# Linear attention and an FFT mixing block on one core: batch 0's DFT without folding, q maxima split in PSUM, V scaled in one tile, key-value copies per pair

## The chip, the cores and the metric

The kernel runs on one core of a Trainium2 chip. A core has five engines that run side by side, each through a queue of its own: TensorE (matmuls; PE in the profile, its weight loads PEld), VectorE (DVE), ScalarE (ACT), GpSimd (POOL) and SyncE (SP, used here to issue DMAs). The metric is the device time of one execution in microseconds (us), the median over runs; less is better.

## The reference

For 8 batches of 8 heads, 576 rows and 64 features per head, the reference computes a linear attention with learned features, then a Fourier mixing and a feed-forward block over the 512 channels that the heads form:

```python
def phi(x):
    proj = np.einsum('bhsd,df->bhsf', x, w_phi)
    proj = proj - np.max(np.abs(proj), axis=-1, keepdims=True)
    return np.concatenate([np.exp(proj), np.exp(-proj)], axis=-1)
q_p, k_p = (phi(q), phi(k))
kv = np.einsum('bhsf,bhsd->bhfd', k_p, v)
z = np.sum(k_p, axis=2)
num = np.einsum('bhsf,bhfd->bhsd', q_p, kv)
den = np.einsum('bhsf,bhf->bhs', q_p, z)[..., None] + 1e-06
...
X = np.fft.fft(x, axis=1)
X = np.fft.fft(X, axis=2)
u = x + np.real(X).astype(np.float32)
mu = np.mean(u, axis=-1, keepdims=True)
var = np.mean((u - mu) ** 2, axis=-1, keepdims=True)
un = (u - mu) / np.sqrt(var + 1e-06)
ch = np.maximum(un @ w_ch1, 0.0) @ w_ch2
return (u + ch).astype(np.float32)
```

The real part of the two transforms is a product with a cosine table on both axes less a product with a sine table on both axes.

## The kernel before

A batch passes through these stages. The names are those of the profile.

- Loads (`KS`, `QS`, `VS`) are issued on POOL's queue, and transposing DMAs on SP's queue make `KT` and `QT` from them. Batch 0 is loaded by SP as float32 into rooms that W2b and HT use later, and TensorE transposes it (`pst`).
- Keys: `psk` is the projection of a pair of heads; ACT takes both exponentials (`KPp`, `KPn`) and DVE the largest magnitude of each row (`MK`). The shift by the maximum is not put into the exponentials of k but into V: POOL multiplies V by exp(MK) and by exp(-MK), into the tiles VCn and VCp (and V4N, V4P for the last 64 rows), whose 65th column holds the scale itself and so yields the denominator.
- Queries: `psh`, `ph` and `psn` are projections, `QPHP` and `QPHN` their exponentials. The maxima of q (`MQ`, from `psq`) enter by a factor on the result (`E2`) in batches 1 to 7. In batch 0 they are turned into rows by `turn_m` (split into three bfloat16 parts on DVE, one matmul `pt` against an identity) and added to the projection on TensorE before the exponential (`negative`).
- `kv` is the key-value product of one head, in PSUM; ACT copies it to `kvh`. `pn` is the product with the query features; the division puts the result into `X`, 128 rows by five groups by 512 channels.
- Folding (`folded`): sums and differences of rows and of channels, on DVE, into `R` and then `CEO`. They use the symmetry of cosine and sine, so that the DFT along rows (`psD`, 12 matmuls, and 3 of `px`) and along channels (`pu`, 12 matmuls) is a quarter of the full one. The sum with `X` stays in `X`.
- Normalising: `UN` is the centred row, `UT` its transpose (`put` on TensorE in batch 0, a DMA in the others). The feed-forward block follows: `psf` with ACT's `HT`, then `pso`, then the store.

The tables of sine and cosine (`SS`, `CS`, `SD`, `CD`) are made on the chip at the start: POOL and DVE reduce the angles, ACT takes the sine. ACT loads a table of functions whenever it changes between sine and exponential.

The order of all this is written out by hand. Each stage is a generator that yields after a step, and the string `PLAN` names with one letter after another whose next step is issued: F the feed-forward, M the mixing with its heads, D the folding, T the exponentials, P the maxima of q, R those of k, S the scaling of V, N and U the normalising, K, V and Q the loads, W the weights' loads, C and H the tables, Z the memsets, G and J the transposes of batch 0's k and q, Y the `stir` steps: four matmuls of ones into a tile that nobody reads (`idle`), fifteen such steps. Every engine runs its part in that order, so an instruction that waits holds all behind it on its engine. `PAIRS` is the order of head pairs in batch 0: outer (0 and 3) first, then inner.

PSUM is cut into three pools: `pj` with 2 tiles of two banks, `pk` with 1, `pb` with 3 of one bank.

## Time and profile before

| what | value |
|---|---|
| median of 3 runs | 417.63 us |
| lowest and highest run | 414.85 and 420.42 us |
| the profiled execution | 415.15 us |
| its span, first to last instruction | 413.4 us |
| mean granted TensorE clock in it | 0.995 |
| HBM read and written | 36.77 and 9.44 MB |

The span is what the trace covers, and all lines of the profile are of that one execution. Its page names the busy time of each engine, but a busy share says little when stages have different limits: the windows of 8 to 32, 32 to 51 and 51 to 403 us have to be read apart. In a row of a timeline stand the start, the duration, the engine, the line, the operation, the tile it writes and those it reads, and in brackets the idle time ahead with what ended it.

### The profile page before, as it was taken

To read this page: it belongs to the slowest core of one execution; us is meant where nothing else is said; L and a number is where in the kernel's file an instruction comes from. 1 tells how busy PE (TensorE), PEld (TensorE's weight loads), DVE (VectorE), ACT (ScalarE), POOL (GpSimd) and SP (SyncE) were. 2 spreads that over 40 slices of the span, in tenths; PEclk is the share of its full clock that TensorE was granted. 3 is DMA by queue.
4 is the path that set the end of the run, shared out by engine and by line. 5 is a ranking of instruction groups with operands and counts; after the bars stand their busy time and mean duration, and the time that the engine had idled before them with its cause. 6 is when DMAs were issued, how large, how long until landed. Compare 5 with 4: busy or idle time off the path is not lost.

```text
span 413.4 us, 10526 instructions
## 1 busy us (share of the span) xinstructions
PE 394.6 (95%) x4194; PEld 259.5 (63%) x4194; DVE 319.4 (77%) x662; ACT 303.8 (73%) x617; POOL 215.1 (52%) x279
## 2 busy tenths in 40 slices
PE   7898999989999989999899999999999999999994
PEld 3574577535856568566756577566856586658563
DVE  5979887999699867797689878888799768875101
ACT  6988999658958886688868886789758885544350
POOL 8997695774466753707658373649271343201000
PEclk9999899999999999999999999999999999999999
DMA  7999979898674899654965979757952141106103
GB/s 210 221 170 158 181 100 185 87 118 128 102 118 58 67 179 141 63 92 83 129 97 65 156 104 142 80 72 116 117 97 52 46 83 21 27 14 114 24 23 90
DMA packets 108520, 42.71 MB, mean 103 GB/s; under 512 B 82615, under 2 KB 103479, under 8 KB 108471
## 3 DMA queue, kind: packets, MB, share of 16 engines
q0 software_dynamic: 46272, 16.60, 37.1%
q1 hardware_dynamic: 61703, 24.85, 32.9%
q10 hardware_dynamic: 496, 0.59, 0.6%
q8 instruction: 33, 0.54, 0.5%
q14 instruction: 16, 0.13, 0.1%
HBM read 36.77 MB, written 9.44 MB: 112 GB/s over the span
## 4 chain that ended last, share of the span: by engine, by line
PE 69%; DVE 13%; DMA 8%; ACT 4%; POOL 3%; issue 2%; DVEq 0%; POOLq 0%; SPq 0%; ACTq 0%
PE psf L1207 29%; PE pso L1224 19%; DMA UT<-UN 4%; PE kv L853 3%; PE psD L1035 2%; PE psk L468 2%; DMA KT<-KS 2%; PE pu L1087 2%; DMA KS<-in_k_dram 2%; PE psq L522 2%; PE psh L563 1%; DVE MK L488 1%; PE pso L1250 1%; DVE cb L969 1%; DVE X L1077 1%
## 5 line engine op out<-in xcount | busy, mean ns | idle before, releaser
L1207 PE MATMUL psf<-UT,W1b 128*128 128x320 bf16 (+1 forms) x1024 | 141.1, 286 | 2.9 <-DMA UT<-UN 2.8
L1224 PE MATMUL pso<-W2b,HT 128*128 128x512 bf16 x496 | 120.5, 379 | 0.0
L1207 PEld LDWEIGHTS <-W1b 128*128 128x128 bf16 x1024 | 94.6, 98 | 30.9 <-issue 3.8
L1212 ACT ACTIVATE HT<-psf 128x320 bf16<-128x320 f32 x128 | 53.9, 444 | 25.7 <-PE psf L1207 19.5
L1224 PEld LDWEIGHTS <-HT 128*128 128x128 bf16 x496 | 45.2, 98 | 43.2 <-issue 0.4
L975 POOL TENSOR_TENSOR X<-cb,rd 128x640 f32<-128x640 f32 x28 | 35.1, 1254 | 52.9 <-DVE rd L973 29.6
L443 POOL TENSOR_TENSOR VCn<-VS,VCn 128x512 bf16<-128x512 bf16 x28 | 29.9, 1067 | 43.4 <-ACT VCn L438 36.6
L530 DVE TENSOR_REDUCE MQ<-psq 128x8 f32<-128x1024 f32 (+1 forms) x32 | 34.3, 1088 | 17.8 <-PE psq L522 17.4
L1230 DVE SCALAR_TENSOR_TENSOR X<-pso,rs,X 128x512 f32<-128x512 f32 x31 | 23.0, 743 | 28.2 <-PE pso L1224 28.0
L1214 ACT ACTIVATE HT<-psf 128x512 bf16<-128x512 f32 x64 | 37.3, 602 | 6.8 <-PE psf L1207 6.6
L488 DVE TENSOR_REDUCE MK<-psk 128x8 f32<-128x1024 f32 x28 | 33.8, 1210 | 1.4 <-ACT KPn L474 1.4
L474 ACT ACTIVATE KPp<-psk 128x1024 bf16<-128x1024 f32 x28 | 28.8, 1027 | 7.8 <-PE psk L468 7.5
L258 POOL DMA_DIRECT2D QS<-in_q_dram x49 | 33.4, 688 | 1.1 <-issue 1.1
L1133 ACT ACTIVATE UN<-X,MV 128x512 bf16<-128x512 f32 (+1 forms) x35 | 25.2, 726 | 11.5 <-DVE MV L1158 8.0
L572 ACT ACTIVATE QPHP<-psh 128x1024 bf16<-128x1024 f32 x28 | 28.9, 1031 | 4.8 <-PE psh L563 4.5
L474 ACT ACTIVATE KPn<-psk 128x1024 bf16<-128x1024 f32 x28 | 28.7, 1025 | 1.7 <-DVE MK L488 1.6
L443 POOL TENSOR_TENSOR VCp<-VS,VCp 128x512 bf16<-128x512 bf16 x28 | 29.9, 1067 | 0.0
L572 ACT ACTIVATE QPHN<-psh 128x1024 bf16<-128x1024 f32 x28 | 29.0, 1036 | 0.0
L1157 DVE BATCH_NORM_STATS2 st<-X 128x6 f32<-128x512 f32 (+1 forms) x40 | 27.1, 678 | 0.2
L1077 DVE TENSOR_TENSOR X<-pu,X 128x512 f32<-128x512 f32 (+3 forms) x49 | 23.5, 526 | 4.6 <-PE pu L1087 4.5
L955 PEld LDWEIGHTS <-QPHP 128*128 128x128 bf16 x280 | 20.5, 99 | 7.8 <-DVE cb L969 3.8
L1173 POOL TENSOR_TENSOR rs<-VE,mhalf 128x5 f32<-128x5 f32 (+1 forms) x9 | 10.3, 1148 | 24.8 <-DVE VE L1172 24.7
(462 smaller groups left out, 797.2 us busy)
## 6 DMA issues: line engine op xcount, KB each, us to landing
out_dram<-X SPq DMA_DIRECT2D x31, 128.0 KB
out_dram<-X SPq DMA_DIRECT2D x15, 256.0 KB
KS<-in_k_dram POOLq DMA_DIRECT2D x7, 512.0 KB, 8.2
VS<-in_v_dram POOLq DMA_DIRECT2D x14, 256.0 KB, 4.8
W1b<-in_moe_w_ch_dram POOLq DMA_DIRECT2D x1, 2048.0 KB, 15.3
W2b<-in_moe_w_ch_dram POOLq DMA_DIRECT2D x1, 2048.0 KB, 16.1
QS<-in_q_dram POOLq DMA_DIRECT2D x28, 64.0 KB, 3.6
QS<-in_q_dram POOLq DMA_DIRECT2D x7, 256.0 KB, 5.6
```

The source lines that it names most:

```text
L258: nc.gpsimd.dma_start(out=pieces[i][0], in_=pieces[i][1])
L443: nc.gpsimd.tensor_tensor(out=VC[:, hs, :, 0:D], in0=values[b][0][:, hs, :].rearrange("p h (j d) -> p h j d", d=D), in1=VC[:, hs, :, D:D + ...
L474: nc.scalar.activation(out=KP[:, hs, :, :].rearrange("p e (jp jj) f -> p jj (e jp) f", jj=2), in_=psk[:], func=AT.Exp, scale=sgn,)
L488: nc.vector.tensor_reduce(out=MK[:, 2 * pr:2 * pr + 2, :].rearrange("p e (jp jj) -> p jj (e jp)", jj=2), in_=tiles[pr][:], axis=AX.X, op=A ...
L530: nc.vector.tensor_reduce(out=o, in_=i[:], axis=AX.X, op=ALU.max, apply_absolute_value=True)
L572: nc.scalar.activation(out=o, in_=psh[:], func=AT.Exp, scale=sgn)
L975: nc.gpsimd.tensor_tensor(out=X[:, :, at:at + 2 * D].rearrange("p c (e d) -> p e c d", e=2), in0=cb[:, :, :, 0:D], in1=rd[:].to_broadcast( ...
L1077: nc.vector.tensor_tensor(out=to, in0=more, in1=to, op=ALU.add)
L1207: nc.tensor.matmul(ps, lhsT=W1b[:, cc, 128 * hh:128 * hh + 128], rhs=UT[:, cc, lo:hi], start=(cc == 0), stop=(cc == NCC - 1),)
L1212: nc.scalar.activation(out=HT[:, hh, lo:hi], in_=ps, func=AT.Relu, scale=-1.0)
L1214: nc.scalar.activation(out=HT[:, hh - 1:hh + 1, lo:hi], in_=psw[:].rearrange("p (a n) -> p a n", a=2), func=AT.Relu, scale=-1.0,)
L1224: nc.tensor.matmul(po[:], lhsT=HT[:, hh, at:at + 128], rhs=W2b[:, hh, :], start=(hh == 0), stop=(hh == NHH - 1),)
```

## The change

It has four parts, and the first half of `PLAN` is written anew for them; behind batch 2 the string is the same letter for letter.

- Batch 0's DFT is done without folding. `less_first` subtracts row 0 from `X` (a matmul `pm` of ones with that row, a subtraction on DVE), in two halves of the channels, into `XB` (bfloat16, in R's room). `first_rows` runs 40 matmuls of 320 columns (for each quarter of the channels, cosine and sine, five groups of rows), and `first_channels` 48 of 256 columns in place of 12. They need a few more tables, products of CD and SD with alternating signs (`full`, `SN`), made on DVE.
- The sines are taken at the start, ahead of the first exponential; the warm-up call of ACT loads the sine table. The angles are reduced on DVE, where POOL did a part. `PAIRS` is now 0, 1, 2, 3, and outer means heads 0 to 3; `stir` has seven steps.
- `turn_m` transposes the float32 maxima three times over in one go and takes the three bfloat16 parts out of PSUM.
- V, in all batches, is scaled into one tile for both signs (VC, V4S): POOL writes the negative of MK beside it, ACT takes one exponential over both, and POOL one product over both. `keyvalue` puts two heads into one PSUM tile, and ACT copies both at once.

On ACT, at the start of the program, the rows ahead of the first exponential of the keys (`KT` is the transposed k of batch 0, `K4p` and `K4n` the features of its last rows, `KPp` those of a pair) were:

```order
L357 CAST wphi_95<-wphi_f 128x128
L350 CAST KT_169<-pst 128x256
L350 CAST KT<-pst 128x512
L761 ACTIVATE K4p<-ps_229 128x512
L762 ACTIVATE K4n<-ps_229 128x512
L776 ACTIVATE KPp<-psk 128x2x4x128
```

and are:

```order
L383 CAST wphi_95<-wphi_f 128x128
L376 CAST KT_168<-pst 128x256
L376 CAST KT<-pst 128x512
L217 ACTIVATE SS<-gs 128x960
L221 ACTIVATE CS<-ga,halfpi 128x960
L226 ACTIVATE SD<-ga 128x512
L228 ACTIVATE CD<-ga,halfpi 128x512
L779 ACT_TABLE_LOAD
L779 ACTIVATE K4p<-ps_224 128x512
```

The four sines and the load of the exponential table moved ahead of batch 0's features; before they stood behind batch 0's last exponential, with a table load on either side:

```order
L690 ACTIVATE QPHN<-ph_739 128x2x2x64
L212 ACT_TABLE_LOAD
L212 ACTIVATE SS<-gs 128x960
L216 ACTIVATE CS<-ga,halfpi 128x960
L221 ACTIVATE SD<-ga 128x512
L223 ACTIVATE CD<-ga,halfpi 128x512
L882 CAST HI_103<-R 1x257
L883 CAST HI_103<-R 1x255
L459 ACT_TABLE_LOAD
```

At that place the last exponential is now followed by the copies of row 0 alone, and batch 1's keys come next.

On DVE, from the last division of batch 0's heads on (`X` is the attention's result), the rows were:

```order
L919 TENSOR_TENSOR X<-pn__794,rd_815 128x2x5x64
L869 TENSOR_TENSOR R<-X 128x2x256 x2
L875 TENSOR_TENSOR R<-X 128x255
L878 TENSOR_TENSOR R<-X 128x1
L875 TENSOR_TENSOR R<-X 128x255
L878 TENSOR_TENSOR R<-X 128x1
L886 TENSOR_TENSOR R<-R 128x2x255 x2
L890 TENSOR_TENSOR R<-R 128x2
L893 SCALAR_TENSOR_TENSOR R<-R 128x2
L998 SCALAR_TENSOR_TENSOR R<-R,keep,pm 65x257
```

and are:

```order
L934 TENSOR_TENSOR X<-pn__768,rd_789 128x2x5x64
L903 TENSOR_TENSOR R<-X,pm 128x2x256 x2
L907 SCALAR_TENSOR_TENSOR R<-X,keep,pm 65x256
L903 TENSOR_TENSOR R<-X,pm 128x2x256 x2
L907 SCALAR_TENSOR_TENSOR R<-X,keep,pm 65x256
L1077 CAST R<-psD 128x320
L520 TENSOR_REDUCE MK_727<-ps_811 128x4
```

The foldings are gone, six subtractions stand in their place, and the results of the row DFT (`psD`) are read out right behind them.

The core of the diff:

```diff
-PAIRS = (0, 3, 2, 1)
+PAIRS = (0, 1, 2, 3)
...
-    "CYCCZYCYGGTRTTGZZGTYZWRTJTSRJGRJYSTPTSPKTTPJMJRTSSKMYMBMPTQPTPQVTMZTMQTMMTPCMMMTTMTHDYAMMYHHDHHKYYVD"
+    "CCYCCGCGZHZHCHHTZGGTHJTKHPQTTJZKRWSRJYTTRGJSSPRTYPTRJTMMYPTSTMMPSTTZPTMPTBKZTMQMMQMHTTHMMVTAMMMDYDYD"
...
+    V4S = const.tile([128, 2, 4, 2, D + 1], BF16, name="V4S")
...
-        nc.scalar.activation(out=warm[:], in_=halfpi[:], func=AT.Exp)
+        nc.scalar.activation(out=warm[:], in_=halfpi[:], func=AT.Sin)
...
+    def scaling(b, MK, MK4, VC):
...
+        def scale_v(pr):
+            if pr % 2 == 0:
+                h4 = slice(2 * pr, 2 * pr + 4)
+                nc.gpsimd.tensor_single_scalar(
+                    out=MK[:, 0, h4], in_=MK[:, 1, h4], scalar=-1.0, op=ALU.mult
+                )
+                nc.scalar.activation(
+                    out=VC[:, :, h4, :, D].rearrange("p s h j -> p s (h j)"),
+                    in_=MK[:, :, h4].rearrange("p s h j -> p s (h j)"), func=AT.Exp, scale=1.0,
+                )
+            hs = slice(2 * pr, 2 * pr + 2)
+            to = VC[:, :, hs].rearrange("p s h j d -> p s (h j) d")
+            nc.gpsimd.tensor_tensor(
+                out=to[:, :, :, 0:D],
+                in0=V[:, hs, :].rearrange("p h (j d) -> p (h j) d", d=D).unsqueeze(1)
+                    .to_broadcast([128, 2, 8, D]),
+                in1=to[:, :, :, D:D + 1].to_broadcast([128, 2, 8, D]), op=ALU.mult,
+            )
...
         def turn_m(outer):
-            m = half(mq[:].rearrange("p (x e) c -> p x (e c)", e=2), outer)
...
+            pt = pk.tile([96, 2, 128], F32, tag="pk", name="pt")
+            m = M0w[:, 1 - outer]
+            nc.scalar.copy(out=m[:, 1:3], in_=m[:, 0:1].to_broadcast([128, 2, 32]))
+            nc.tensor.transpose(pt[:, 0], m.rearrange("p i n -> p (i n)"), ident[:])
...
-            nc.vector.tensor_copy(out=mt_[:], in_=pt[:])
+            nc.vector.tensor_copy(out=mt_[:], in_=pt[:, 0])
+            nc.vector.tensor_tensor(
+                out=pt[0:64, 1], in0=pt[0:64, 0], in1=mt_[0:64], op=ALU.subtract
+            )
+            nc.vector.tensor_copy(out=mt_[0:64], in_=pt[0:64, 1])
...
     def keyvalue(b, h):
...
+        if e == 0:
+            pool, tag = (pb, "pb") if b == 0 else (pk, "pk")
+            two_heads[b] = pool.tile([128, 2, 2, D + 1], F32, tag=tag, name="kv")
+        kv = two_heads[b][:, e]
...
+        if e:
+            kvh = work.tile([128, 2, 2, D + 1], BF16, tag="kvh", name="kvh", bufs=4)
+            nc.scalar.copy(out=kvh[:], in_=two_heads[b][:])
+            return kvh[:, 0], kvh[:, 1]
+        return ()
...
+    def less_first(X, XB):
...
+        for outer in (True, False):
+            qs = slice(0, 2) if outer else slice(2, 4)
+            nc.scalar.copy(out=HI[0:1, qs], in_=XQ[0:1, 4, qs])
+            pm = pb.tile([128, 2, 128], F32, tag="pb", name="pm")
+            nc.tensor.matmul(pm[:], lhsT=ones_b[:], rhs=HI[:, qs], start=True, stop=True)
+            yield
+            for cs in (slice(0, 2), slice(2, 4)):
+                nc.vector.tensor_tensor(
+                    out=XBQ[:, cs, qs], in0=XQ[:, cs, qs],
+                    in1=pm[:].unsqueeze(1).to_broadcast([128, 2, 2, 128]), op=ALU.subtract,
+                )
...
+    def first_rows(XB, EO):
+        for quarter in range(4):
+            for i in range(2):
+                ps = pb.tile([128, 512], F32, tag="pb", name="psD")
+                for c in range(5):
+                    deep = 65 if c == 4 else 128
+                    mat = (SS if c in (2, 3) else SN) if i else CS
+                    nc.tensor.matmul(
+                        ps[:, 0:NK], lhsT=XB[0:deep, c, 128 * quarter:128 * quarter + 128],
+                        rhs=mat[0:deep, 2 if c == 4 else c % 2, :], start=(c == 0), stop=(c == 4),
+                    )
+                if i:
+                    nc.scalar.copy(out=EO[:, i, quarter, :], in_=ps[:, 0:NK])
+                else:
+                    nc.vector.tensor_copy(out=EO[:, i, quarter, :], in_=ps[:, 0:NK])
+                yield
+
+    def first_channels(t, pu, EO):
...
+        todo = [(quarter, i, n) for quarter in range(4) for i in range(2) for n in range(2)]
+        for z, (quarter, i, n) in enumerate(todo):
+            nc.tensor.matmul(
+                pu[0:M, n, :], lhsT=EO[:, i, quarter, 128 * t:128 * t + M],
+                rhs=tables[quarter][n][i], start=(z == 0), stop=(z == len(todo) - 1),
+            )
...
     def stir(b):
-        for i in range(15):
+        for i in range(7):
```

329 lines of the change are left out of this document (146 added, 183 removed).

## The prediction, made before the result was known

> **What bounds the kernel now.** I read the page's busy shares first, then windows by stage, then the waits of TensorE from the middle on, and last the timelines of ACT, DVE and PE up to 51 us.
>
> ```profile
> PE 394.6 (95%) x4194; PEld 259.5 (63%) x4194; DVE 319.4 (77%) x662; ACT 303.8 (73%) x617; POOL 215.1 (52%) x279
> ```
>
> The average says TensorE. The windows (PE, PEld, DVE, ACT, POOL busy us, then clock and DMA) say where it is not TensorE alone:
>
> ```profile
> 8.00:32.00 24.00, 21.25 (x321) 14.69 (x321) 21.48 (x41) 22.43 (x47) 22.80 (x28) 1.00 1.04 206
> 32.00:51.00 19.00, 16.23 (x146) 8.64 (x145) 17.24 (x46) 17.50 (x30) 14.11 (x25) 0.91 1.49 169
> 51.00:84.00 33.00, 32.62 (x412) 22.29 (x411) 28.73 (x66) 29.36 (x62) 23.37 (x26) 1.00 1.04 128
> 84.00:121.00 37.00, 35.19 (x390) 22.48 (x389) 32.54 (x62) 27.99 (x58) 21.93 (x27) 1.00 0.75 115
> 121.00:403.00 282.00, 278.11 (x2859) 185.18 (x2859) 213.87 (x431) 202.00 (x416) 126.78 (x151) 1.00 0.60 84
> ```
>
> From 51 us on TensorE is busy 345.92 of 352 us. Work that leaves ACT, DVE or POOL there buys nothing unless it ends a TensorE wait. The longest TensorE waits, for 50 to 121 us and then for 121 us to the end (us in total, times, longest), are:
>
> ```profile
> PE psD L1035 <- DVE CEO L1007: 1.2, 1, 1.2
> PE psD L1035 <- DVE CEO L1053: 0.4, 1, 0.4
> ```
> ```profile
> PE psf L1207 <- DMA UT<-UN: 2.8, 4, 1.3
> ```
>
> So the time is the moment at which TensorE gets its first `psf` matmul (batch 0's feed-forward) plus the TensorE work that is left then. Before that moment TensorE is filled with dummy matmuls. The same windows, counting only `idle` (PE busy, clock, DMA):
>
> ```profile
> 8.00:32.00 24.00, 3.97 (x16) 1.00 1.04 206
> 32.00:51.00 19.00, 7.95 (x29) 0.91 1.49 169
> 51.00:121.00 70.00, 1.04 (x4) 1.00 0.88 121
> ```
>
> In 32 to 51 us, 7.95 of 16.23 busy us are filler: this is the room into which the change puts the unfolded DFT. What sets the first `psf` is a chain: ACT's exponentials of batch 0, then DVE's folding, then DFT and transposes.
>
> ```profile
> 7.59 0.58 ACT L350 CAST KT<-pst 128x512 bf16<-128x512 f32 x1 [0.21 <-PE pst L345]
> 8.07 0.60 ACT L761 ACTIVATE K4p<-ps 128x512 bf16<-128x512 f32 x1
> 31.52 0.39 ACT L690 ACTIVATE QPHN<-ph 128x256 bf16<-128x256 f32 x1
> 31.93 1.28 ACT L212 ACT_TABLE_LOAD   x1
> 33.23 1.00 ACT L212 ACTIVATE SS<-gs 128x960 bf16<-128x960 f32 x1
> 35.64 0.71 ACT L223 ACTIVATE CD<-ga,halfpi 128x512 bf16<-128x512 f32 x1
> 38.06 1.28 ACT L459 ACT_TABLE_LOAD   x1 [0.20 <-PE ps L454]
> ```
> ```profile
> 34.10 0.82 DVE L919 TENSOR_TENSOR X<-pn__794,rd 128x640 f32<-128x640 f32 x1
> 42.76 0.17 DVE L1053 CAST CEO<-R 128x6 bf16<-128x6 f32 x1
> ```
> ```profile
> 40.07 0.40 PE L468 MATMUL psk<-wphi,KT 64*128 64x128 bf16 x8 [1.76 <-DMA KT<-KS]
> 40.40 1.63 PE L1019 MATMUL psD<-SS,CEO 128*128 128x289 bf16 x6
> 43.97 0.91 PE L1019 MATMUL psD<-CS,CEO 128*128 128x289 bf16 x6
> 44.72 0.54 PE L1058 MATMUL px<-CS,CEO 128*128 128x289 bf16 x3
> 45.91 0.27 PE L1087 MATMUL pu<-CD,DT 128*128 128x256 bf16 x1 [0.33 <-DVE DT L1030]
> 46.02 0.27 PE L1087 MATMUL pu<-SD,ET 128*128 128x256 bf16 x1
> 50.90 0.82 PE L1207 MATMUL psf<-UT,W1b 128*128 128x256 bf16 x6
> ```
>
> ACT runs from 8.07 to 31.91 us almost without a pause, `X` is whole at 34.92, DVE folds until 42.93, the channel DFT `pu` starts at 45.91 and `psf` at 50.90.
>
> **The change, part by part.**
>
> Prices of what is merged or added come from these groups (mean ns of one):
>
> ```profile
> L861 ACT CAST kvh<-kv 128x130 bf16<-128x130 f32 x64 | 17.4, 276 | 2.7 <-PE kv L857 2.6
> L438 ACT ACTIVATE VCn<-MK 128x16 bf16<-128x16 f32 x14 | 4.0, 287 | 0.4 <-DVE MK L488 0.3
> L424 ACT ACTIVATE V4N<-MK 64x4 bf16<-64x4 f32 x14 | 3.0, 216 | 0.4 <-DVE MK L483 0.2
> L639 ACT ACTIVATE QPHP<-psh 128x512 bf16<-128x512 f32 x4 | 2.3, 662 | 0.0
> L648 ACT ACTIVATE QPHP<-psh 128x1024 bf16<-128x1024 f32 x2 | 2.1, 1070 | 0.0
> ```
> ```profile
> L443 POOL TENSOR_TENSOR VCn<-VS,VCn 128x512 bf16<-128x512 bf16 x28 | 29.9, 1067 | 43.4 <-ACT VCn L438 36.6 <-issue 2.8 <-ACT VCp L438 2.7
> L428 POOL TENSOR_TENSOR V4N<-VS,V4N 64x256 bf16<-64x256 bf16 x14 | 8.7, 618 | 22.4 <-ACT V4N L424 18.5 <-PE psf L1207 3.4
> L233 POOL TENSOR_SCALAR CD<-CD 1x256 bf16<-1x256 bf16 x1 | 1.2, 1205 | 0.1
> L510 POOL MEMSET MQ<- 64x4 f32 x7 | 0.7, 99 | 0.4
> ```
> ```profile
> L1048 DVE SCALAR_TENSOR_TENSOR R<-pm,R 128x514 f32<-128x514 f32 x8 | 5.5, 685 | 0.0
> L998 DVE SCALAR_TENSOR_TENSOR R<-R,keep,pm 65x257 f32<-65x257 f32 x8 | 3.8, 474 | 1.8 <-PE pm L994 1.8
> L488 DVE TENSOR_REDUCE MK<-psk 128x8 f32<-128x1024 f32 x28 | 33.8, 1210 | 1.4 <-ACT KPn L474 1.4
> ```
>
> *1. Sines to the front.* The four sines move from behind the last exponential to a place between ACT's second `KT` copy and `K4p`. From 33.23 to 36.35 they take 3.1 us; with one table load behind them (1.28) `K4p` moves back by 4.4 us. One of the three table loads goes, because the warm-up call now loads the sine table. Their inputs come from DVE instead of POOL; ACT needs them only after 8 us, when before's DVE had them nearly done, so I cost that at nothing; if `ident`, now formed behind two table steps on DVE, is late, the first transposes and all of ACT are late with it.
>
> *2. Fewer ACT instructions in batch 0.* V's last-row scales 4 to 2: -2 x 0.22. Its other scales 4 to 2: -2 x 0.29. Copies of `kvh` 8 to 4, twice as wide: a saving between 0 (time all in the width) and 4 x 0.276 = 1.1, I take 0.5. Outer features 8 x 512 to 4 x 1024 columns: 4 x (2 x 0.66 - 1.07) = -1.0. The splitting of q's maxima in PSUM adds two small copies on ACT, between 0.1 and 0.28 each: +0.4. Sum -2.1; back-to-back ACT instructions overlap a little, so -1.6. ACT's last `QPHN` then ends at 31.9 + 4.4 - 1.6 = 34.7 us, and `X`, 3.0 us behind it now, at 37.7 (before 34.92). DVE has the small table products in this stretch as well; they lie under ACT's exponentials.
>
> *3. Folding out, subtraction in.* Before, 34.92 to 42.93 is folding (with one MK reduction inside). Now per half of the columns: two 128x512 subtractions and one of 65 rows, 2 x 0.685 + 0.474 = 1.84 us. Only the first half stands ahead of the first `psD`: 39.5 us. The second runs under the first half's matmuls.
>
> *4. DFT unfolded.* Along rows 8 groups of 5 matmuls of 320 columns. Six of 289 take 44.72 - 43.97 = 0.75 us, 0.125 each, so 320 take 0.138: 40 x 0.138 = 5.5 us. Along channels 48 of 256 columns at 46.02 - 45.91 = 0.11: 5.3 us. Before: 15 x 0.125 + 12 x 0.11 = 3.2 us. So TensorE gets 7.6 us more, and 32 filler matmuls less, at about 1.04/4 = 0.26 us: -8.3. As a total this cancels; what counts is the place. Between the first `psD` and `psf` the order also has three `psk`, one `psq` and one `psh` group (0.40 each by the `psk` row), two transposes of four matmuls (0.25 each, taken from 0.125 by two) and 4 fillers (1.04), about 3.1 us. First `psf` at 39.5 + 5.5 + 5.3 + 3.1 = 53.4 us, 2.5 later than before. The results of `psD` leave by ACT and DVE in turn; that is hidden as long as each leaves in under 1.4 us. If MK's 1.21 us stands in front, one group waits: 0 to 1.5 us, I take 0.
>
> *5. What is left behind the first `psf`.* The filler in the window 51 to 121 (1.04 us) is gone, one `psq` and one `psh` group are already done (0.40 us for 8 small matmuls, by the `psk` row, and about the same): -1.8 us. DVE has one MK (1.21) and one pair of q maxima of batch 1 behind it earlier, and batch 1's folding is not interrupted by them. That can end the 1.2 + 0.4 us that `psD` waits for CEO; it can also only move them, so 0 to -1.6, I take -0.8.
>
> *6. The seven other batches.* ACT loses per batch 2 x 0.22 + 2 x 0.29 + about 0.5 for the copies, 1.5 us. POOL's two 1.07 us products become one of twice the width, between 1.07 and 2.14 us, nearest to 2.13; the small sign flips are new and lie between 0.10 (smallest memset) and 1.2 us (the one-row TENSOR_SCALAR), three a batch. None of it is on TensorE, which has no wait on `kvh` or VC in the list after 51 us. 0 us, both ways at most the 1 us that a late VC could cost.
>
> **Sum** against the profiled execution (span 413.4, time 415.15): +2.5 - 1.8 - 0.8 = -0.1, so 415.0. That execution lies 2.5 us below the median of 417.63; the same shift would give 417.5. I say 415.5, with most weight on the execution the rows come from.
>
> A word on fillers. In the rows, six `psD` took 1.63 us after a pause of 1.76 and 0.91 us a little later; the window's granted clock is 0.91. So a pause of that size cost 0.7 us; the eight fillers between the two `pm` keep the gap there below it, so the sum holds no term for it. The Trainium skill (TensorE: Matmul & The Clock Gate, Part 1: The HAM clock gate) says that the clock falls to half after an idle window of about 3.4 us and takes as long a busy one to come back; in the rows here a shorter pause sufficed. By that rule the start, with 4 fillers in place of 12, would run its first transposes at half speed, an estimate of 1 us more, so 416.0 where the sum has 415.0.
>
> **Rivals.**
>
> *A. As summed, a wash.* 411 to 420. Chance 0.62.
>
> *B. The front does not get later.* The sines could sit in time that ACT loses anyway to DVE's maxima, and the room that the unfolded DFT fills is free. If `X` ends at 35.5 instead of 37.7 and the 1.6 us of CEO waits go entirely: 415.15 + 0.3 - 1.8 - 1.6 = 412.0. For over 2% (406.8 on this execution's scale) `psf` would have to start near 46 us, which needs the first `psD` at 32, before `X` exists even now. Against it: ACT's 22.43 busy of 24 us from 8 to 32. Chance 0.26, of it 0.11 beyond 2%.
>
> *C. POOL's queue holds batch 0, slower.* V's products start only after their scales, which ACT issues 4 us later, and POOL now has six loads of batch 1's K and Q ahead of them beside W1b's. Four products of 2.1 us and the flips end near 30.5 us if a flip costs 0.2, and near 33.5 if it costs 1.2. Heads 6 and 7's `kv` stand on TensorE ahead of the last `psn`; beyond about 32 us each us goes straight into `X`. At 33.5: +1.5 to +3, so 417 to 418; over 2% needs them past 40, which takes slow issues too. Chance 0.12, of it 0.06 beyond 2%.
>
> **Chances.** Faster by over 2%, 0.11 (B's end); slower by over 2%, 0.07 (C's end and 0.01 of A); within 2%, which is about what runs that spread from 414.85 to 420.42 can tell, 0.82. The range: below, B at 412.0 and as much again for the unknown ends of terms 4 and 5, 408; above, C at 418 plus the skew of 2.5 between execution and median and 1.5 of stall, 422.
>
> **What would show it.** In the new profile: ACT's sines at 8 to 12 us and only two table loads; `K4p` near 12.5; last `QPHN` near 34.7; first `psD` near 39.5, `psf` near 53.4; no wait of `psD` on CEO in 50 to 121. Wrong would be: `K4p` before 10 or `psf` before 51 (B), or `kv` waiting for VC around 30 us (C).

## The result: slower by 0.7 per cent

After: 418.18 us median of 20 runs (417.52 to 428.13). Before, run beside it: 417.49 us (413.73 to 425.46). The ratio is 1.0073 with a 95% interval of 1.0053 to 1.0093. It leaves out executions in a slower state, over 1.5 per cent above the kernel's fastest (six of before's 20 and one of after's), and so lies above the ratio of the two medians. The prediction said 415.5, with -0.1 us as the sum of the change; it is about +3. The time lies in the stated 408 to 422 and within 2 per cent of before, as the largest chance had it; that it did not come there by the stated sum is shown below. The profiled execution of after took 417.52 us with a span of 415.7 (before: 415.15 and 413.4).

The windows of after, with the bounds shown of before (busy us of PE, PEld, DVE, ACT, POOL, then clock, DMA share, GB/s):

```profile
8.00:32.00 24.00, 20.56 (x223) 13.88 (x223) 18.51 (x32) 21.42 (x34) 15.58 (x20) 0.93 1.11 207
32.00:51.00 19.00, 17.94 (x254) 12.68 (x255) 15.78 (x36) 14.18 (x25) 11.86 (x18) 1.00 0.96 106
51.00:84.00 33.00, 32.33 (x423) 24.94 (x422) 25.31 (x69) 28.36 (x54) 22.08 (x25) 1.00 1.09 138
121.00:403.00 282.00, 275.73 (x2834) 184.59 (x2857) 215.07 (x434) 202.00 (x383) 128.94 (x138) 1.00 0.62 87
```

ScalarE has less to do from 32 to 51 us (14.18 for 17.50 us), as the change meant, and TensorE from 51 us on is as full as before. TensorE's granted clock from 8 to 32 us fell from 1.00 to 0.93; from 14 to 26 us, where it was 0.86, ScalarE was busy 11.92 of 12 us, so the chain did not wait for it there. So the difference is in when TensorE gets batch 0's feed-forward. The same chain as in the prediction, of after, on ScalarE, VectorE and TensorE:

```profile
9.77 0.59 ACT L376 CAST KT<-pst 128x512 bf16<-128x512 f32 x1 [0.67 <-PE pst L371]
13.39 1.28 ACT L779 ACT_TABLE_LOAD   x1
14.68 0.60 ACT L779 ACTIVATE K4p<-ps 128x512 bf16<-128x512 f32 x1
27.87 1.02 ACT L668 ACTIVATE QPHP<-psh 128x1024 bf16<-128x1024 f32 x1 [0.96 <-PE psh L660]
33.43 1.94 ACT L668 ACTIVATE QPHP<-psh 128x1024 bf16<-128x1024 f32 x2 [0.73 <-PE psh L660]
37.84 0.38 ACT L710 ACTIVATE QPHN<-ph 128x256 bf16<-128x256 f32 x1
```
```profile
40.21 0.82 DVE L934 TENSOR_TENSOR X<-pn__768,rd 128x640 f32<-128x640 f32 x1
```
```profile
42.55 0.86 PE L1070 MATMUL psD<-CS,R 128*128 128x320 bf16 x5
57.46 0.61 PE L1247 MATMUL psf<-UT,W1b 128*128 128x256 bf16 x4
```

Step by step, the length of each piece of this chain (us):

| piece | before | predicted for after | after |
|---|---|---|---|
| start to `K4p` | 8.07 | 12.5 | 14.68 |
| `K4p` to the end of the last `QPHN` | 23.84 | 22.2 | 23.54 |
| to `X` whole | 3.01 | 3.0 | 2.81 |
| to the first `psD` | 5.48 | 1.8 | 1.52 |
| to the first `psf` | 10.50 | 13.9 | 14.91 |
| first `psf` at | 50.90 | 53.4 | 57.46 |
| from there to the end of the span | 362.5 | 359.9 | 358.2 |

The first `psf` came 4.1 us later than predicted, and 1.7 of that were made up behind it. Where can be followed from output to output: each row of this kind on VectorE (the feed-forward's sum into `X`) is one finished tile. First of before, then of after, the fifth, and the last of these 31:

```profile
83.28 0.74 DVE L1230 SCALAR_TENSOR_TENSOR X<-pso,rs,X 128x512 f32<-128x512 f32 x1
121.13 0.70 DVE L1230 SCALAR_TENSOR_TENSOR X<-pso,rs,X 128x512 f32<-128x512 f32 x1
402.14 0.75 DVE L1230 SCALAR_TENSOR_TENSOR X<-pso,rs,X 128x512 f32<-128x512 f32 x1 [11.40 <-PE pso L1224]
```
```profile
88.09 0.74 DVE L1270 SCALAR_TENSOR_TENSOR X<-pso,rs,X 128x512 f32<-128x512 f32 x1
124.42 0.70 DVE L1270 SCALAR_TENSOR_TENSOR X<-pso,rs,X 128x512 f32<-128x512 f32 x1
405.40 0.75 DVE L1270 SCALAR_TENSOR_TENSOR X<-pso,rs,X 128x512 f32<-128x512 f32 x1 [11.40 <-PE pso L1264]
```

After is 6.6 us behind at the first `psf`, 4.8 at the first tile, 3.3 at the fifth and 3.3 at the last. The span is only 2.3 us longer, because from the end of VectorE's last instruction, with the last store behind it, 4.4 us are left in this execution and 5.4 in that of before. TensorE's waits in after from 50 to 121 us (in total, times, longest) no longer hold the two on CEO, 1.6 us, that before had:

```profile
PE psk L505 <- DVE MK L525: 1.5, 1, 1.5
PE psf L1247 <- DVE MQ L567: 0.4, 2, 0.2
```

The wait of 1.5 us for `MK` is new, so these lists come out even. Nor is there in after any wait of `psf` for the transposing DMA (`UT<-UN`), which cost before 2.8 us behind the fifth tile; other waits there took their place (1.3 us for `MQ`, 0.8 each for `kvh` and `KPn`), and the lag at the end is that at the fifth tile. From here on "lag" means the start of such a row less that of before.

### The profile page after: what moved, and what is told of

Its sections match the earlier page's. It is cut to its first block, busy times and chain, and to the rows that moved or that the text cites. A ratio compares the mean times of both kernels' runs of the same rounds, so it can differ in the third digit from the quotient of the medians.

```text
span 415.7 us, 10465 instructions
## 1 busy us (share of the span) xinstructions
PE 391.2 (94%) x4195; PEld 265.3 (64%) x4224; DVE 317.5 (76%) x658; ACT 297.7 (72%) x548; POOL 208.1 (50%) x251
## 4 chain that ended last, share of the span: by engine, by line
PE 75%; DVE 12%; ACT 5%; POOL 3%; issue 2%; DMA 1%; POOLq 0%; DVEq 0%; ACTq 0%
PE psf L1247 27%; PE pso L1264 20%; PE pso L1290 4%; PE kv L844 4%; PE psD L1031 3%; DVE MQ L567 2%; PE pu L1127 2%; PE psk L505 2%; PE psq L559 2%; PE psh L600 1%; PE psD L1070 1%; POOL X L989 1%; DVE cb L983 1%; DVE R L862 1%; PE idle L1362 1%
## 5 line engine op out<-in xcount | busy, mean ns | idle before, releaser
L1264 PE MATMUL pso<-W2b,HT 128*128 128x512 bf16 x467 | 117.2, 379 | 2.1 <-issue 1.0
L462 POOL TENSOR_TENSOR VC<-VS,VC 128x1024 bf16<-128x1024 bf16 x28 | 53.8, 1932 | 39.1 <-ACT VC L456 37.7
L567 DVE TENSOR_REDUCE MQ<-psq 128x8 f32<-128x1024 f32 (+1 forms) x32 | 34.3, 1086 | 14.1 <-PE psq L559 13.9
L444 POOL TENSOR_TENSOR V4S<-VS,V4S 64x512 bf16<-64x512 bf16 x14 | 14.9, 1061 | 23.2 <-ACT V4S L441 21.7
```

The source lines that it names most:

```text
L462: nc.gpsimd.tensor_tensor(out=to[:, :, :, 0:D], in0=V[:, hs, :].rearrange("p h (j d) -> p (h j) d", d=D).unsqueeze(1) .to_broadcast([128, ...
L567: nc.vector.tensor_reduce(out=o, in_=i[:], axis=AX.X, op=ALU.max, apply_absolute_value=True)
L1264: nc.tensor.matmul(po[:], lhsT=HT[:, hh, at:at + 128], rhs=W2b[:, hh, :], start=(hh == 0), stop=(hh == NHH - 1),)
```

## The experiments

Each ran beside the kernel before on the same chip. The ratios are of time to before, with 95% intervals; `psf` and `K4p` are the starts in the profiled execution. e2 and e7 hold e1's edit too, and e16 that of e15.

| run | K4p | first psf | lag, first / fifth / last tile | ratio to before |
|---|---|---|---|---|
| after | 14.68 | 57.46 | 4.8 / 3.3 / 3.3 | 1.0073 (1.0053 to 1.0093) |
| e1 ident first | 13.47 | 56.24 | 3.6 / 2.1 / 3.6 | 1.0083 (1.0047 to 1.0118) |
| e2 and warm | 13.56 | 56.83 | 4.2 / 2.7 / 5.3 | 1.0103 (1.0064 to 1.0142) |
| e7 angles on GpSimd | 14.45 | 57.22 | 4.6 / 3.1 / 3.1 | 1.0062 (1.0028 to 1.0096) |
| e14 memsets late | 13.16 | 56.42 | 3.8 / 2.3 / 2.2 | 1.0029 (0.9993 to 1.0064) |
| e13 both, ident and memsets | 12.90 | 56.15 | 3.5 / 2.0 / 2.4 | 1.0026 (1.0002 to 1.0050) |
| e15 and a sine ahead | 12.08 | 55.55 | 2.9 / 1.4 / 4.3 | 1.0050 (1.0020 to 1.0079) |
| e16 and the turns reordered | 12.12 | 55.66 | 3.0 / 1.5 / 2.4 | 1.0020 (0.9996 to 1.0044) |

### The late start: e1, e2, e7, e14, e13

In after the transposes of k wait for `ident`, which VectorE makes behind five angle steps (three products and two steps on 128x960). e1 makes it first:

```diff
         count(tn, [[1, 128]], 0, -1)
+        nc.vector.tensor_single_scalar(out=ident[:], in_=tn, scalar=0.0, op=ALU.is_equal)
...
         )
-        nc.vector.tensor_single_scalar(out=ident[:], in_=tn, scalar=0.0, op=ALU.is_equal)
         nc.vector.tensor_copy(out=ident_b[:], in_=ident[:])
```

> The changed kernel, with the identity (ident) formed on DVE ahead of the angle steps, as before. Theory F (the loss is made at the front: TensorE's first transpose waits until 8.01 us for ident, then runs at half clock): the first transposes near 6.5 us in place of 8.01, K4p near 13.1 in place of 14.68, first psf near 56.0 in place of 57.46, ratio to before near 1.0035 in place of 1.0073. Rival D (the 7.6 us of added DFT work on TensorE are the loss, and what comes before them has slack): ratio stays within 0.001 of 1.0073.

`K4p` came 1.2 us earlier and stopped there, since a sine now waits for its angle, made by VectorE (ScalarE of e1):

```profile
10.91 0.63 ACT L226 ACTIVATE SD<-ga 128x512 bf16<-128x512 f32 x1 [0.78 <-DVE ga L207]
13.47 0.60 ACT L779 ACTIVATE K4p<-ps 128x512 bf16<-128x512 f32 x1
```

The time did not change, which was rival D's sign. At the fifth tile 1.2 us are still there, then they go; of that below. e2 adds eight fillers at the start (the head of `PLAN`, and two more steps of `stir`):

```diff
-CCYCCGCG
+CCYYYCCGCG
...
-        for i in range(7):
+        for i in range(9):
```

> As the one before, and 8 more filler matmuls at the very start (12 as before the change). Theory F: the transposes also run at full clock, KT's copy on ACT near 7.8 us in place of 9.77, K4p near 12.5, first psf near 55.3, ratio near 1.002. Rival: the fillers only occupy TensorE, and the ratio is that of the kernel with ident first.

With them eight transposes took 1.09 us where e1 and after needed 1.97, so the slow start of TensorE is real (the granted clock does not show it: 1.00 from 6.5 to 10.2 us in e1 and in e2); but `K4p` stood at 13.56, because here the angles set it (and the twelve fillers held the first transpose until 6.75; e1: 5.92). In after, where the sines follow the copies of `KT` without a pause, it counts. The first transposes, of before and then of after:

```profile
6.51 0.46 PE L345 MATMUL pst<-ident,HT 64*128 64x64 f32 x4
```
```profile
8.01 0.68 PE L371 MATMUL pst<-ident,HT 64*128 64x64 f32 x4 [5.03 <-DVE ident L168]
```

From this start to the second copy of `KT` it is 1.08 us in before (7.59) and 1.76 in after (9.77). So `ident` makes this copy 1.5 us late and the slow transposes another 0.7. e7 tried the angles: products back on GpSimd.

```diff
-            nc.vector.tensor_scalar(
+            nc.gpsimd.tensor_scalar(
                 out=turns[:, NK * j:NK * j + NK], in0=rs, scalar1=pn[:, j:j + 1], scalar2=MAGIC,
```

> The kernel after with ident formed first and the three products of the angles (0.99 us each on VectorE beside GpSimd's counting) back on GpSimd, as before. Theory D (VectorE's chain of angles sets the sines, and through them K4p): K4p at about 12.7 (13.5 with ident first, 14.7 after), first psf at about 55.5 (56.2, 57.5), time 1.005 to 1.008 of before. Rival: the products take as long on GpSimd behind its counting, and K4p stays at 13.3 or later.

The expectation fell: `K4p` at 14.45, later than with ident first alone. Why is in the rows, first of GpSimd (the first and the last of five memsets in a row), then of VectorE in e7:

```profile
5.27 0.52 POOL L263 MEMSET QPHP<- 128x512 bf16 x1
6.50 0.52 POOL L268 MEMSET V4S<- 128x520 bf16 x1
```
```profile
5.24 2.29 DVE L189 TENSOR_SCALAR gs<-gs 128x960 f32<-128x960 f32 x1 [1.79 <-POOL gs L183]
```

The step on 128x960 took 2.29 us beside the memsets, to 7.53, half a microsecond past their end at 7.02; in after, where GpSimd is idle by then, it took 0.66. In before one memset stood beside it, and it took 0.94, ending as in e7 0.51 us past the memset:

```profile
5.82 0.53 POOL L242 MEMSET QPHP<- 128x512 bf16 x1
```
```profile
5.92 0.94 DVE L186 TENSOR_SCALAR gs<-gs 128x960 f32<-128x960 f32 x1 [1.73 <-POOL gs L181]
```

And in after the three products on 128x320 took 2.96 us together, beside GpSimd's counting and memsets (to 5.4 us). e14 and e13 moved the memsets (three Z of `PLAN` behind the fifth H, the memsets of the sines), e14 with nothing else changed:

```diff
-CCYCCGCGZHZHCHHTZGGTHJ
+CCYCCGCGHHCHHTGGTHZZZJ
```

> The kernel after with the three groups of memsets moved alone, ident at its place behind the angles. Theory B: ident formed at about 6.3 us instead of 7.7, first transposes at 6.6 (8.0), K4p at 13.2 (14.7), first psf at 56.0 (57.5). Rival C: K4p within 0.4 us of 14.7.

> The kernel after with ident formed first and GpSimd's three groups of early memsets (3.5 to 5.4 us) moved behind the memsets of the sines. Theory B (VectorE's angle steps are held up while GpSimd writes: 128x320 took 0.99 us beside it, 128x960 took 2.29 us beside its memsets in the run with the products on GpSimd and 0.66 us alone): the three products take about 0.3 us each, the sines never wait for an angle, K4p at 12.6 (13.5 with ident first alone; predicted for after: 12.5), last exponential of QPHN at 36.1, first psf at 55.4. Rival C (VectorE is slow there for its own reasons): K4p at 13.3 or later. The time: 1.002 to 1.006 of before if the gain holds to the end, over 1.006 if the later stages take it back again.

VectorE and ScalarE of after, then of e14:

```profile
2.61 2.96 DVE L183 TENSOR_SCALAR gs<-ga,pn 128x320 f32<-128x320 f32 x3 [0.50 <-POOL ga L155]
7.74 0.22 DVE L168 TENSOR_SCALAR ident<-gs 128x128 f32<-128x128 f32 x1
```
```profile
2.61 1.33 DVE L183 TENSOR_SCALAR gs<-ga,pn 128x320 f32<-128x320 f32 x3 [0.50 <-POOL ga L155]
6.20 0.22 DVE L168 TENSOR_SCALAR ident<-gs 128x128 f32<-128x128 f32 x1
13.16 0.60 ACT L779 ACTIVATE K4p<-ps 128x512 bf16<-128x512 f32 x1
```

The same three instructions, with the same inputs, took 1.33 instead of 2.96 us, and `K4p` came at 13.16 (13.2 expected). So VectorE was slow because of GpSimd's memory clearing beside it. e14's first transpose began at 6.47, 1.5 us earlier than in after, and the slow transposes stayed (1.77 us to the second copy of `KT`). e13 has both edits, `K4p` at 12.90, 0.4 us later than the predicted 12.5. At the last tile the lag is 2.2 and 2.4 us (after 3.3), and the ratios are 1.0029 and 1.0026. Of the two, only e13's interval lies wholly below that of after. How much of this the earlier start brought is not shown: e1 had its first `psf` at the same time as these two (56.24; 56.42 and 56.15) and kept nothing. The Trainium skill (SBUF — State Buffer, SBUF: two separate sides) says that VectorE and GpSimd share a pair of memory ports, which the one that starts first holds for its whole instruction while the other waits, where VectorE's instruction runs in a mode that uses two ports or, beside a GpSimd operation that reads, has two inputs. The rows agree for these instructions, 0.66 us alone, 0.94 beside one memset and 2.29 beside five; in which mode they ran no row says.

### Sines late, and folding back: e3, e4

e3 moves eight H steps, the sines and their products, back behind the last exponential and the warm-up to the exponential table; e4 folds batch 0 again, in after's order of the rest.

```diff
-CCYCCGCGZHZHCHHTZGGTHJTKHPQ...MQMHTTHMMVTAM
+CCYCCGCGZZCTZGGTJTKPQ...MQMTTMMVTHHHHHHHHAM
...
-        nc.scalar.activation(out=warm[:], in_=halfpi[:], func=AT.Sin)
+        nc.scalar.activation(out=warm[:], in_=halfpi[:], func=AT.Exp)
```
```diff
-        folds[0] = less_first(X, XB)
+        folds[0] = folded(X, R, HI, False)
...
-            yield from first_rows(XB, EO)
+            yield from folded_rows(b, R, CEO, HI)
...
-            if b == 0:
-                first_channels(t, pu, EO)
-            else:
+            if True:
```

> The changed kernel, with the four sines (and the table products behind them) moved back behind batch 0's last exponential, the warm-up call on the exponential table. Theory F: K4p near 10.3 us, X whole near 36.7 in place of 41.03; the sines then end near 38.2, so the first psD comes near 39.5 in place of 42.55 and psf near 54.5; ratio 1.000 to 1.002. Rival S (the sines have to be paid ahead of psD wherever they stand, with one table load more when late): psD and psf as in the changed kernel or 1.3 us later, ratio 1.007 to 1.010.

> The changed kernel with batch 0's DFT folded again (folding on DVE, 15 + 12 matmuls); order, sines, V part stay. Theory F: folding takes about 8 us on DVE from X at 41.03, the unfolded way takes as long on TensorE, so first psf within 1.5 us of 57.46 and ratio within 0.004 of 1.0073, with 7.6 us less TensorE work. Rival D: psf 4 us or more earlier and ratio below 1.000.

Both were much slower, 1.0471 (1.0427 to 1.0514) and 1.0361 (1.0311 to 1.0411), outside what either theory or rival had. In e3 the features start at 10.5 us, but the rest of the order is made for late features. TensorE's waits from 8 to 57 us in e3:

```profile
PE pm L900 <- ACT HI L898: 6.1, 1, 6.1
PE pst L371 <- DVE ident L168: 5.2, 1, 5.2
PE kv L844 <- POOL VC L462: 4.9, 1, 4.9
```
```profile
49.05 0.43 DVE L237 TENSOR_TENSOR ga<-CD,flip 128x512 bf16<-128x512 bf16 x1 [4.32 <-ACT CD L228]
52.38 0.82 DVE L934 TENSOR_TENSOR X<-pn__768,rd 128x640 f32<-128x640 f32 x1
```

The key-value sums wait 4.9 us for V, and on VectorE (the second fence) the table products stand ahead of the last divisions into `X` and wait 4.32 us for the late sines. `X` is whole at 53.2, the first `psf` comes at 73.01. In e4 `X` is whole at the same time as in after, 41.0, but the first `psf` 5.2 us later, and TensorE waits from 36 to 130 us for the folding and its neighbours:

```profile
PE psD L1016 <- DVE MK L511: 3.2, 1, 3.2
PE pm L992 <- ACT HI L862: 3.1, 1, 3.1
PE put L1167 <- ACT UN L1152: 1.9, 1, 1.9
```

A later wait of 6.0 us of `psf` for `UT<-UN`, at 205 to 211 us, makes up most of the rest of its lag (16.5 us at the end). What follows: neither the early sines nor the unfolded DFT can be taken out of this order at a gain. What either is worth in an order made for it, these runs do not tell.

### The turns of q's maxima: e6, e8, e12

Of the 1.6 us by which the chain from `K4p` on was to shrink, 0.3 came: ScalarE's busy time in it fell from 22.29 to 21.33 us, and idle time rose, 0.96 and 0.73 us ahead of two `QPHP` (rows of after above). Ahead of both stands a `turn_m`: ScalarE's copy, a transpose on TensorE, four steps on VectorE, with the next `psh` behind the transpose. e6 takes the copy to VectorE and issues those `psh` ahead of the turns:

```diff
-            nc.scalar.copy(out=m[:, 1:3], in_=m[:, 0:1].to_broadcast([128, 2, 32]))
+            nc.vector.tensor_copy(out=m[:, 1:3], in_=m[:, 0:1].to_broadcast([128, 2, 32]))
...
-TMMYPTSTMMPSTTZPTMPTBKZT
+TTMMPYSTMMPSTTZPTMTPBKZT
```

> The kernel after, with the widening copy of q's maxima on VectorE instead of ScalarE, the second exponential of QPHP issued ahead of the first turn of the maxima, and the third ahead of the second turn. Theory P (ping-pong: ScalarE's idle 0.96, 0.31 and 0.73 us and its two copies of 0.25 us at 26.6 to 33.4 us are what the prediction's saving of 1.6 us lost): last exponential of QPHN ends at about 36.2 (after: 38.2), X whole at 39 (41.0), first psf at 55.6 (57.5), and the time at 1.002 of before (1.000 to 1.005), against 1.007 for after. Rival L (a gain ahead of the first expert product is lost again later, as 1.2 us was in the run with ident formed first): first psf earlier by as much, the end as after, 1.007. Rival N: ScalarE waits for the products of the maxima anyway, and the last exponential ends within 0.7 us of 38.2.

It was slower, 1.0138 (1.0097 to 1.0180), the last `QPHN` ending 3.5 us later. The cause is a side effect of the edit, on TensorE:

```profile
27.53 0.29 PE L716 MATMUL pt<-ident,M 128*96 128x128 f32 x1
29.15 1.86 PE L1362 MATMUL idle<-ones_b 128*128 128x512 bf16 x4 [1.33 <-DVE mt L723]
30.95 0.39 PE L693 MATMUL ph<-QT,wphi 64*128 64x256 bf16 x2
```

The filler writes into the one tile of `pk`, which the turn ahead of it still reads: a dummy waited 1.33 us and then ran four matmuls in 1.86 (1.03 in after), with batch 0's own products behind it. e8 had the same fault beside ident first and the angles on GpSimd (its edit is those of e1, e7 and e6 together):

> The kernel after with all three: ident formed first, the angles' products on GpSimd, the maxima's copy on VectorE with the exponentials moved ahead. Theory: the gains add, K4p at 12.7, last exponential of QPHN at 34.5 (predicted for after: 34.7), first psf at 53.8 (predicted 53.4), and the time at 0.997 to 1.003 of before, as the prediction's sum had it. Rival L (gains ahead of the first expert product are lost later): first psf at 53.8 and the time still over 1.004.

1.0147 (1.0102 to 1.0192), with `K4p` at 14.47 as in e7, so nothing to learn but the same. e12 puts the filler ahead, and has ident first; the copy is on VectorE as in e6:

```diff
-PTRJTMMYPTSTMMPSTTZPTMPTBKZT
+TRPJTYMMTPSTMMPSTTZPTMTPBKZT
```

> The kernel after with ident formed first, the widening copy of the maxima on VectorE, the last key maximum ahead of the last maxima of q, the filler between ahead of the key-value sums, and the second and fourth exponentials of QPHP issued ahead of the turns of the maxima (the last run of this kind had a filler behind the turn, which wrote the tile that the turn still read and waited 1.33 us). Theory P (the turns of the maxima stretched the first part): last exponential of QPHN at 35.5 (37.0 with ident first alone), first psf at 54.8 (56.2). Of the time: by theory L (a gain ahead of the first expert product is lost again later) 1.006 or more, else 1.003 or less.

`K4p` at 13.49 and the end of the last `QPHN` at 37.14 (e1: 13.47 and 37.00). The idle time ahead of `QPHP` is gone, and idle time ahead of `QPHN` has come, for the maxima that the turn makes (ScalarE's waits of e1, then of e12, in this chain):

```profile
ACT QPHP L668 <- PE psh L660: 1.7, 2, 1.0
```
```profile
ACT QPHN L668 <- PE psn L683: 1.4, 2, 0.7
ACT QPHP L710 <- PE ph L693: 0.4, 1, 0.4
ACT QPHP L668 <- PE psh L660: 0.2, 1, 0.2
```

So the ping-pong moves and doesn't end; theory P falls in its size (35.5 expected). The ratio is 1.0072 (1.0037 to 1.0108), as by theory L. Its profiled execution, at 423.18 us above the median of its runs, 418.12, has a stall of 4.05 us that is told below.

### V in one tile and copies by pairs: e5, e9, e10, e11

For batches 1 to 7 the prediction costed this part at 0. e5 is the kernel before with that part alone, batches 1 to 7.

```diff
+                nc.gpsimd.tensor_single_scalar(
+                    out=MK[:, 0, h4], in_=MK[:, 1, h4], scalar=-1.0, op=ALU.mult
+                )
...
-            kv = pk.tile([128, 2, D + 1], F32, tag="pk", name="kv")
+            two_heads[b] = pool.tile([128, 2, 2, D + 1], F32, tag=tag, name="kv")
```

> The kernel before with only the V part of the change, in batches 1 to 7: V's scale with both signs in one tile, one product where there were two, two heads' key-value sums in one PSUM tile with one copy. Batch 0 keeps its own operations. Theory V0 (the part is off the path, as the prediction costed it): the same time as before, ratio 0.997 to 1.003. Rival V+ (the one product of 1.93 us on GpSimd where two of 1.07 us stood, or the copy that waits for the second head, holds back the key-value sums): ratio over 1.003 and longer waits of TensorE for VC. Rival V- (65 narrow instructions fewer on ScalarE and GpSimd shorten each batch): ratio under 0.997.

1.0214 (1.0147 to 1.0281): it costs about 2 per cent in that order. The lag is 1.5 us at the first tile, 5.9 at the fifth. GpSimd and then ScalarE of e5 show a place:

```profile
88.66 2.43 POOL L258 DMA_DIRECT2D QS<-in_q_dram  x4
91.06 1.27 POOL L258 DMA_DIRECT2D VS<-in_v_dram  x2
92.40 0.25 POOL L427 TENSOR_SCALAR MK<-MK 128x16 f32<-128x16 f32 x1
```
```profile
92.69 0.35 ACT L430 ACTIVATE VC<-MK 128x32 bf16<-128x32 f32 x1 [4.95 <-POOL MK L427]
92.83 0.70 ACT L1059 CAST ET<-psD 128x578 bf16<-128x578 f32 x1
```

A sign flip of 0.25 us stands behind 3.7 us of DMA issuing, and ScalarE, with the copy of `psD` behind, waits 4.95 us for it. e9 makes the flips on VectorE, right behind the maxima (in `kmax`):

```diff
-                nc.gpsimd.tensor_single_scalar(
-                    out=MK[:, 0, h4], in_=MK[:, 1, h4], scalar=-1.0, op=ALU.mult
-                )
...
+                nc.vector.tensor_single_scalar(
+                    out=MK[:, 0, hs], in_=MK[:, 1, hs], scalar=-1.0, op=ALU.mult
+                )
```

> The V part alone in the kernel before (2.1 per cent slower), with the two sign flips of a batch made on VectorE right behind the maxima they read, instead of on GpSimd. Theory Q (GpSimd's queue: the flip of 0.25 us waits behind GpSimd's DMA issues from 88.7 to 92.3 us, and ScalarE waits 4.95 us for it with an exponential of the keys and the copies of the transform's first stage behind it): no such wait, time at 1.000 of before (0.996 to 1.005). Rival W (the wide product on GpSimd, 2.25 us for 128x1024, or the copy by pairs is what costs): still over 1.012.

The wait is gone, and the ratio is 1.0172 (1.0135 to 1.0208), rival W's sign: the loss is still there. That doesn't decide against theory Q, because the cure has a price of its own: a flip takes 0.42 us on VectorE, `psD` waits 3.0 us for CEO in e9 (before 1.6 in two waits), and in e11 below the same flips cost 1.6 per cent in the new order. By what waits the V part costs time in the old order stays open. Two more runs in the new order:

> The kernel after with its V part undone in all batches: two exponentials and two products by sign, one copy for each head, in after's order of the rest. Theory O (in after's order the V part costs nothing, since no DMA issue stands ahead of the flips there): the time of after, 1.007 of before (1.003 to 1.011). Rival G (the V part still costs time in the new order): at 1.003 or below. Rival S (the V part saves time in the new order, where ScalarE has 65 narrow instructions fewer): 1.012 or more.

> The kernel after with the sign flips on VectorE behind the maxima, all batches. Theory O: nothing is won where nothing waits for them, 1.007 of before (1.004 to 1.010), the values for the key-value sums of batch 0 about 0.3 us earlier. Rival G: waits of ScalarE for flips are left in the order after, and the time falls to 1.003 or below.

e10 undoes the part in all batches:

```diff
-                    in_=MK[:, :, h4].rearrange("p s h j -> p s (h j)"), func=AT.Exp, scale=1.0,
+                        out=VC_[:, h4, :, D:D + 1], in_=MK[:, 1, h4].unsqueeze(3),
+                        func=AT.Exp, scale=sgn,
...
-            two_heads[b] = pool.tile([128, 2, 2, D + 1], F32, tag=tag, name="kv")
+        kv = pool.tile([128, 2, D + 1], F32, tag=tag, name="kv")
```

1.0257 (1.0223 to 1.0291), rival S: here the part saves 1.8 per cent. The last `QPHN` ends 2.7 us later than in after, the first `psf` comes 3.5 later, and at the fifth tile it is 9.7 us behind after, at the last 8.2. TensorE's waits of e10 from 50 to 130 us begin with:

```profile
PE kv L837 <- ACT kvh L845: 5.4, 7, 1.4
```

The new order runs the key-value sums of two heads back to back; with one PSUM tile for each head, the second waits for the first one's copy. e11 (the edit of e9, made in after and for all batches) was slower too, 1.0238 (1.0198 to 1.0277): its 39 flips of 0.33 to 0.45 us stand on VectorE, whose busy time rose from 317.5 to 334.6 us, and by the third tile it is 6.1 us behind after.

So the part costs 2 per cent in one order and saves nearly as much in the other. It is not wholly the same part: e5 has it in batches 1 to 7, and of the 8.2 us that e10 loses, 3.5 are there at the first `psf`, in batch 0. The part and the new `PLAN` are one edit.

### The rest: e15, e16

e15 starts from e13 and moves one sine (SS) ahead of ScalarE's copies of the transposes. e16 adds the edits of e12.

```diff
-CCYCCGCGHHCHHT
+CCYCCHGCGHCHHT
```

> The kernel of the run with ident first and the memsets late, with one sine (SS) issued ahead of the transposes' copies, in ScalarE's idle 1.12 and 0.67 us there. Theory F (the time after follows the start of the key exponentials, at about 0.7 of each us): K4p at 12.1 (12.9), first psf at 55.4 (56.15), time at 1.000 to 1.002 of before. Rival L (later stages take it up): 1.003 or more.

> As the run before it, and with the reordered turns of q's maxima (copy on VectorE, exponentials moved ahead). Theory F: last exponential of QPHN another 0.2 us earlier, the time as with the sine ahead alone or 0.001 under it. Rival T (PE then runs the first part in an order that starves the key-value sums or the fillers): 0.003 or more above it.

In e15 `K4p` and `psf` came as expected, 12.08 and 55.55, and at the sixth tile the lag is 1.4 us. The time did not: 1.0050, rival L's sign. In e16 the last `QPHN` ended 0.1 us later than in e15 (36.42 and 36.31), not 0.2 earlier, and the ratio was 0.003 lower. Behind the sixth tile, in e15, TensorE waits 2.95 us for a transposing DMA:

```profile
129.84 5.61 PE L1247 MATMUL psf<-UT,W1b 128*128 128x320 bf16 x40 [2.95 <-DMA UT<-UN]
```

Such waits over the whole execution (us, times) and the first `psf`: after none at 57.46; e7 none at 57.22; e2 3.7, 2 at 56.83; e14 1.3, 1 at 56.42; e1 1.1, 2 at 56.24; e13 1.6, 1 at 56.15; e16 2.1, 2 at 55.66; e15 4.1, 2 at 55.55. All runs of this list that begin before 57 us have such waits, but e2 shows that their length does not follow the start alone. In e15 these two DMAs were issued at 121.9 us, in after at 122.9, so 1.0 us sooner, where the fifth tile came 1.9 us sooner; in both they stood behind three transposes into `QT` on the same queue, and the DMA share from 127 to 130 us was 1.58 (after 0.96). Why TensorE waited so long for this one is not shown. In e16, 1.8 us at the first `psf` were worth 0.9 us at the end (against after, last tile 2.4 and 3.3).

No run beat the kernel before. The best of them, e16 at 1.0020 (0.9996 to 1.0044), is not told apart from it, and neither is e14.

## Why the prediction was wrong

Its picture held: TensorE's first `psf` plus what is left then sets the time, the sines go to the front with two table loads in all, and rival C did not come: `kv` has one wait in after, of 0.77 us, which the profile puts down to VectorE's maxima. The sum was wrong, by terms 1 and 2 above all; 1.7 us of the miss came back behind the first `psf` by what no term had, which was luck.

1. *Sines to the front*, +4.4, measured +6.6. The arithmetic of the sines was right (3.1 us and one load of 1.28). The step that failed is "their inputs come from DVE instead of POOL ... I cost that at nothing". Its reason was that before's VectorE was nearly done with them by 8 us; in the rows its last step for SS and CS ended at 9.41, and that for SD and CD at 28.5. What cost time was another thing: GpSimd did the products in before and had a single memset beside VectorE's step; without the products its five memsets came in a row from 3.53 us on (before: the first at 5.82, the others behind 11.5), beside VectorE's. The warning in that sentence (`ident` late, then all of ScalarE late) is what happened, for 1.5 of the 2.2 us, and e14 takes just these 1.5 away. The other 0.7 are the slow first transposes, which the sum had left out (last paragraph). e13 cures 1.8 of the 2.2, and e15 shows that the rest can be had by filling ScalarE's gap.
2. *Fewer ACT instructions*, -1.6, measured -0.3. The instructions did shrink by 1.0 us of busy time (2.1 predicted before the overlap, 1.6 behind it); 0.7 came back as waits. The step assumed that ScalarE alone is the chain since it was 22.43 of 24 us busy. Once it has less to do, `turn_m`'s round over three engines is as long; e12 moved the wait and ended nothing.
3. *Subtraction in*, 1.84 to the first `psD`, measured 1.52. Right.
4. *DFT unfolded*, 13.9 from `psD` to `psf`, measured 14.9. The matmuls cost what was said; the rest between them is 4.1 and not 3.1 us. Of this 0.4 is a slip in the prediction: the pieces that it names, five groups of 0.40, two transposes of 0.25 and 1.04 of fillers, add up to 3.5.
5. *Behind the first `psf`*, -2.6, measured -4.3: 3.3 up to the fifth tile, nothing from there to the last, and 1.0 in the last store. The waits on CEO went, but a wait of 1.5 us for `MK` came, so the 0.8 taken for them was not won there ("it can also only move them"). The fillers and groups that the term names are 1.8 by its own prices; what else made up the 3.3 is not broken down. The 1.0 at the store is a difference of two single executions.
6. *The seven other batches*, 0. As a total it stands: from the fifth tile on, the lag stays within 1 us. The reason given was wrong. Off TensorE is not off the path: the part alone costs 2.1 per cent in the old order, and its absence 1.8 in the new one (batch 0 included), by waits that the list of before could not show.

Taken together, 2.2 and 1.3 us from terms 1 and 2, 1.0 from 4 and -0.5 from smaller pieces make the 4.1 us at the first `psf`; with -1.7 behind it, +2.4 against the sum. That term 1 failed at the memsets is shown by e14, in `K4p`. In the time it is shown only in part: e13 stands at 1.0026, with 0.9 us less lag than after at the last tile, and e1, as early at `psf`, did not gain. Where the loss that is left in e13, 0 to 0.5 per cent, lies was not found; terms 2 and 4 were not cured.

The sentence on the cold start, by the Trainium skill (TensorE: Matmul & The Clock Gate, Part 1: The HAM clock gate), gave 1 us more. The trace agrees in kind: the slow transposes came (1.97 us for eight, 1.09 with fillers). They cost about 0.7 us of `K4p` in after, an estimate from the 1.76 and 1.08 us above. No run has warm transposes in an order where the angles don't hold the sines, so this part was not cured by itself.

## What to carry to other kernels

When work moves from one engine to another, look at what the engine that gave it up does next, and beside whom: here GpSimd's memsets came 2.3 us earlier and made VectorE's steps there more than twice as long. A part taken out of (or put into) an order written by hand measures the part and the misfit together; only the pair of runs, with it and without it in both orders, tells them apart. A filler is not free if its tile is one that real work reads.

## What the runs showed of the hardware

- VectorE beside GpSimd's memsets: 128x960 in 2.29 us beside five, 0.94 beside one (ending 0.51 us past the last memset in both cases), 0.66 alone; three of 128x320 in 2.96 against 1.33, with GpSimd's counting beside them in both.
- Eight transposes on TensorE took 1.97 us behind four fillers (e1, after) and 1.09 behind twelve (e2), with a granted clock of 1.00 in the profile of both.
- In e12 TensorE stopped in the middle of a row of equal matmuls for 4.05 us, with no releaser that the profile shows, while the DMA share was 1.77 (32 to 40 us) and 1.70 (40 to 46):

```profile
37.27 0.19 PE L925 MATMUL pn__744<-kvh,QPHN 128*128 128x65 bf16 x1
41.51 0.23 PE L925 MATMUL pn__744<-kvh,QPHP 128*128 128x65 bf16 x1 [4.05 <-issue]
```

The granted clock was 0.50 from 40 to 46 us. In e2 the same kind of wait at that place was 0.7 us. What held TensorE there is not shown.
